# A one-core transformer block on Trainium2: a new order for every job, with new banks and copy engines

## The chip, the cores and the metric

One core of a Trainium2 chip runs the kernel. The metric is the device time of one execution in microseconds, from its start to its end. The engines are TensorE (PE, matmuls and their weight loads), VectorE (DVE), ScalarE (ACT), GpSimd (POOL) and SyncE (SP), whose queue issues all DMAs of this kernel. SBUF is the on-chip memory, and PSUM, 8 banks of 128x512 f32, takes what TensorE writes.

## The reference

Two residual blocks on x of 2048 tokens and 448 columns, bf16. The first is attention with 16 heads of 28 columns, where each token sees 8 keys, at distances 0, 2, ..., 14 behind it. The second is a gated MLP whose gate is mixed over the tokens by a 2048x2048 matrix.

```python
x = A_x
h = x + _A_ref(_layernorm(x, axis=-1), A_wqkv, A_wo)      # attention over 8 keys, then @ wo
h2 = h + _B_ref(_layernorm(h, axis=-1), B_w_in, B_w_sp, B_b_sp, B_w_out)

def _B_ref(x, w_in, w_sp, b_sp, w_out):
    z = _gelu(jnp.einsum('bsd,df->bsf', x, w_in))          # 1792 columns
    z1 = z[..., :Fh].copy()                                # Fh = 896
    z2 = _layernorm(z[..., Fh:], axis=-1)
    g = jnp.einsum('ts,bsf->btf', w_sp, z2) + b_sp[None, :, None]
    return jnp.einsum('bsf,fd->bsd', z1 * g, w_out)
```

## The kernel before

The 2048 tokens are 16 tiles of 128, numbered 0 to 15. In the order of the data, the stages are:

1. *First layer norm*, a tile at a time: statistics on VectorE (L607, tile `st1`), their aggregate (L609, `mv1`), the reciprocal root on GpSimd (L601, L602, `rs`, for groups of one, two or four tiles), and the normalisation on VectorE (L618), which writes `xn`, a ring of six places. The name `n0_5` is the normalisation of tile 5 in layer norm 0.
2. *Transposes of `xn` into `xhT`*: tiles 0 to 3 on TensorE (L647) with an evacuation from PSUM, the others by a DMA from SP's queue (L519).
3. *Projections* (L495, function `product`): queries and keys for five stretches of tokens (256, 256, 512, 512, 512) in four groups of heads each, and V for each attention block. Each product is two jobs, A and B, on half arrays of 64 rows (64\*128 in the profile); another job must stand between them. A function `move` (L505) copies each out of PSUM, on ScalarE or VectorE. The same function makes the padded weights `wqk` out of `wraw` at the start; GpSimd clears their padding (L668).
4. *Attention*, in 18 blocks of 128, 112 or 114 tokens: logits (L763), exponential on ScalarE (L772, tile `E`), the multiplication by the mask on VectorE (L778), the product with V (L787), a reciprocal (L795) and a multiplication (L798) on VectorE into `otm`, a small copy of `otm` (L505), and a DMA transpose into `OT` (L519; through `OTs` and one more copy for blocks that end off a boundary). Then the output projection (L495) and the residual add on VectorE, two tiles at a time (L731), into `x_tm`.
5. *Second layer norm* of these, like the first, and a DMA transpose into `hnT`.
6. *Gate half of the MLP*, for each tile: product (L495), for some tiles a raw copy out of PSUM (L505) with the gelu behind it (L836), for others the gelu straight from PSUM (L839), two halves of statistics (L843, `st3`), aggregate (L846), root on GpSimd, normalisation (L852) into `z2p`.
7. *Other half* (L495 and gelu L880), into `z1p`.
8. *Spatial product* (L908): 28 groups of 16 matmuls of 128x512 with `wsp_la`, `wsp_hi`, `wsp_lb` as weights' sides and the normalised gate `z2p`; then an add of the bias (L917) and the gate's multiplication (L920) on VectorE.
9. *Last projection* (L932), residual add (L939) and the store of the result (L520).

These stages overlap widely: while the attention of later tokens runs, the MLP of the earlier ones has begun. Nothing decides this while the kernel runs or is built: every job (912 of them) has a number, and three lists written out at the top of the file hold the whole arrangement. `ORDER` is the order of all jobs. Each engine issues its own in this order, and waits by semaphores where an operand or a bank isn't ready. The number 912 in it stands for one filler matmul on a constant tile (L947, `warm`). `BANK` has the first PSUM bank of each product in the order in which the products were declared, and `ON` the engine of each copy that may go to either of two.

```python
for t, b in zip(self.tickets, BANK):      # L301
    t.b = b
for i in ORDER:
    j = self.jobs[i]
    out.append(j)
...
eng = ON.get(name, eng)                   # L504, in move
```

Names of copies in `ON`: `xe` evacuates a transpose of `xn`, `wp` pads weights, `qe2_1` evacuates group 1 of the third stretch of queries and keys, `ve` V of a block, `od` copies `otm`, `oc` copies from `OTs` to `OT`, `z2c5` is the raw copy of tile 5's gate.

Of the kernel before, what the change touches and what calls it, by code (L numbers as in the profile page):

```python
# [25 lines left out]
ORDER = [21, 36, 112, 24, 22, 25, 0, 37, 38, 1, 44, 45, 35, 39, 40, 46, 47, 2, 116, 3, 121, 23, 912, 912, 912, 912, 912, 912,  # L26
# [200 lines left out]
class Planner:  # L227
# [69 lines left out]
    def order(self):  # L297

        ready, out = {}, []
        left = [j.ndep for j in self.jobs]  # L300
# [707 lines left out]
```

## Time and profile before

| | |
|---|---|
| three runs | 240.85, 243.95, 241.71 us; median 241.71 |
| profiled execution | 240.89 us, its span 239.2 us |
| TensorE busy | 231.4 us (97%), 2099 matmuls |
| TensorE weight loads | 114.3 us (48%), 2110 |
| VectorE busy | 152.3 us (64%), 323 instructions |
| ScalarE busy | 92.0 us (38%), 113 |
| GpSimd busy | 35.2 us (15%), 73 |
| DMA | 23.26 MB, mean 97 GB/s |

The span runs from the first to the last instruction of the profiled execution; the time has 1.7 us more around it. Weight loads overlap matmuls. An engine's share is a mean over all stages, so it doesn't tell which stage waits for what: for that, the profile is read by stretches of time.

In the rows of the profile, a time line reads: start, duration, engine, line, operation, output and inputs, the number of instructions in the row, and in brackets the idle time ahead of it and what released it. The chain of waits is followed back from the last instruction.

### The profile page before, as it was taken

What the parts mean: (1) busy time and instruction counts of PE and PEld (TensorE: products, weight loads), DVE (VectorE), ACT (ScalarE), POOL (GpSimd) and SP (SyncE); (2) the same over time, 40 slices, a digit from 0 to 9 for tenths busy, and PEclk for the clock granted to TensorE, in tenths of its full rate; (3) what the DMA queues carried; (4) which work ended last, traced back from release to release, by engine and by line L of the source; (5) the groups of instructions that cost most, each with busy time, mean ns of one, the idle gap of its engine ahead of it and who ended that gap; (6) DMA issues with size and microseconds to landing.
All of it is one profiled execution on the core that took longest, in us unless ns stands there. A gap on an engine that the chain in (4) does not pass through costs nothing.

```text
span 239.2 us, 4969 instructions
## 1 busy us (share of the span) xinstructions
PE 231.4 (97%) x2099; PEld 114.3 (48%) x2110; DVE 152.3 (64%) x323; ACT 92.0 (38%) x113; POOL 35.2 (15%) x73
## 2 busy tenths in 40 slices
PE   7989999799999999999999999999999999999995
PEld 2564464354555644444444444444444444444453
DVE  5799799979989987959877124410751222613674
ACT  3787988768789656687820000000000000000000
POOL 5154220440302030313124000000000000000000
DMA  6943538526668967979999970000000010000032
GB/s 202 340 119 69 137 70 142 89 60 124 148 106 165 171 108 157 154 149 165 168 192 166 186 189 0 3 0 0 0 0 3 31 47 0 0 3 0 26 108 97
DMA packets 66310, 23.26 MB, mean 97 GB/s; under 512 B 58608, under 2 KB 66160, under 8 KB 66288
## 3 DMA queue, kind: packets, MB, share of 16 engines
q1 hardware_dynamic: 66288, 22.95, 47.1%
q8 instruction: 16, 0.26, 0.4%
q14 instruction: 6, 0.05, 0.1%
HBM read 6.83 MB, written 1.84 MB: 36 GB/s over the span
## 4 chain that ended last, share of the span: by engine, by line
PE 81%; DVE 9%; DMA 4%; ACT 2%; SPq 2%; issue 1%; POOL 0%
PE psum L908 40%; PE psum L495 27%; PE psum L932 9%; DMA x_tm<-in_A_x_dram 3%; PE psum L763 2%; PE psum L787 2%; DVE st L607 2%; DVE E L778 2%; DMA xhT<-xn 2%; ACT E L772 1%; DVE z2p L505 1%; DVE otm L798 1%; SPq L520 1%; SPq L519 1%; DVE xn L618 1%
## 5 line engine op out<-in xcount | busy, mean ns | idle before, releaser
L908 PE MATMUL psum<-wsp_hi,z2p 128*128 128x512 bf16 x218 | 50.6, 379 | 0.3
L917 DVE TENSOR_TENSOR ub<-psum,bb 128x512 bf16<-128x512 f32 x28 | 19.2, 689 | 44.4 <-PE psum L908 43.9
L772 ACT ACTIVATE E<-psum 128x896 bf16<-128x896 f32 (+2 forms) x36 | 32.0, 934 | 9.0 <-PE psum L763 9.0
L908 PEld LDWEIGHTS psum<-wsp_hi,z2p 128*128 128x128 bf16 x224 | 21.9, 98 | 26.1
L495 PE MATMUL psum<-xhT,wqk 64*128 64x512 bf16 (+1 forms) x280 | 27.1, 334 | 2.0 <-DMA xhT<-xn 1.6
L908 PE MATMUL psum<-wsp_lb,z2p 128*128 128x512 bf16 x108 | 26.1, 379 | 0.2
L908 PE MATMUL psum<-wsp_la,z2p 128*128 128x512 bf16 x111 | 25.9, 379 | 0.2 <-issue 0.2
L495 PE MATMUL psum<-w_in,hnT 64*128 64x448 bf16 x224 | 24.8, 349 | 0.1
L495 PE MATMUL psum<-hnT,w_in 64*128 64x512 bf16 x196 | 24.1, 376 | 0.0
L939 DVE TENSOR_TENSOR srg<-psum,x_tm 128x448 bf16<-128x448 f32 (+1 forms) x17 | 9.7, 592 | 20.8 <-PE psum L932 20.7
L932 PE MATMUL psum<-w_out,z1p 128*128 128x448 bf16 (+1 forms) x119 | 22.3, 341 | 0.0
L843 DVE BATCH_NORM_STATS2 st<-z2p 128x6 f32<-128x448 bf16 x32 | 18.9, 609 | 3.7 <-ACT z2p L836 3.4
L778 DVE TENSOR_TENSOR E<-E,maskb 128x1792 bf16<-128x1792 bf16 (+2 forms) x18 | 19.6, 1095 | 1.7 <-ACT E L772 1.6
L607 DVE BATCH_NORM_STATS2 st<-x_tm 128x6 f32<-128x448 bf16 x32 | 19.4, 612 | 1.6 <-DMA x_tm<-in_A_x_dram 1.4
L602 POOL TENSOR_TENSOR rs<-rs,negh 128x2 f32<-128x2 f32 (+2 forms) x22 | 18.9, 857 | 1.8
L495 PEld LDWEIGHTS psum<-xhT,wqk 64*128 64x128 bf16 x280 | 12.8, 94 | 12.3 <-ACT E L772 2.4
L908 PEld LDWEIGHTS psum<-wsp_la,z2p 128*128 128x128 bf16 x112 | 10.9, 98 | 13.4 <-DVE z2p L852 0.4
L908 PEld LDWEIGHTS psum<-wsp_lb,z2p 128*128 128x128 bf16 x112 | 11.0, 98 | 13.2
L932 PEld LDWEIGHTS psum<-w_out,z1p 128*128 128x128 bf16 x119 | 11.6, 98 | 10.2 <-DVE z1p L920 0.3
L880 ACT ACTIVATE z1p<-psum 128x1024 bf16<-128x1024 f32 x14 | 14.2, 1023 | 5.2 <-PE psum L495 5.1
L495 PEld LDWEIGHTS psum<-w_in,hnT 64*128 64x128 bf16 x224 | 10.6, 94 | 11.0 <-DVE z2p L505 0.6
L601 POOL TENSOR_SCALAR rs<-mv 128x2 f32<-128x2 f32 (+2 forms) x22 | 6.3, 288 | 62.1 <-DVE mv L609 41.3
(54 smaller groups left out, 226.2 us busy)
## 6 DMA issues: line engine op xcount, KB each, us to landing
w_in<-in_B_w_in_dram SPq DMA_DIRECT2D x8, 224.0 KB, 3.0
out_dram<-srg SPq DMA_DIRECT2D x16, 112.0 KB, 1.7
x_tm<-in_A_x_dram SPq DMA_DIRECT2D x3, 448.0 KB, 6.1
wraw<-in_A_wqkv_dram SPq DMA_DIRECT2D x2, 448.0 KB, 4.1
w_out<-in_B_w_out_dram SPq DMA_DIRECT2D x1, 784.0 KB, 6.4
bb<-in_B_b_sp_dram SPq DMA_DIRECT2D x1, 512.0 KB, 5.8
wv<-in_A_wqkv_dram SPq DMA_DIRECT2D x2, 224.0 KB, 6.3
wo<-in_A_wo_dram SPq DMA_DIRECT2D x1, 336.0 KB, 7.7
```

What stands on the lines that cost most here:

```text
L495: ins = e.matmul(out(k), w(k, p0, c), x(k, p0, c), start=(k, p0, c) in first, stop=(k, p0, c) in last, tile_position=(p0, 0))
L601: [(lambda e: e.tensor_single_scalar(A, mv[:, m:m + n, 1], EPS, ALU.add), r_mv[k][m:m + n], [rr]), (lambda e: e.tensor_tensor(R, A, negh[: ...
L602: (lambda e: e.tensor_tensor(R, A, negh[:, 0:1].to_broadcast([128, n]), ALU.pow), [rr, r_negh], r_rs[k][m:m + n])],
L607: [(lambda e: e.bn_stats(st[:, m, :], src), [rsrc], [r_st[k][m]])], dve_t(D))
L772: return e.activation(o, i, AF.Exp, scale=SCALE)
L778: return e.tensor_tensor(a, a, maskb[:, 0:1, pad:pad + nq].to_broadcast([NK, NHEAD, nq]), ALU.mult)
L843: [(lambda e, m=m, k=k: e.bn_stats(st3[:, m, k, :], z2p[:, m, D * k:D * (k + 1)]), [r_z2[m]], [r_st[2][m]])], dve_t(D))
L880: return e.activation(o, i, AF.Gelu_apprx_tanh)
L908: ins = e.matmul(psv(tk), z2p[:, s, 128 * fc:128 * fc + 128], w[:, 512 * (tc % 2):512 * (tc % 2) + 512], start=(s == 0), stop=(s == NB - 1))
L917: [(lambda e, tc=tc, s=s, tk=tk: e.tensor_tensor(ub[:, s, :], psv(tk), bb[:, 512 * tc:512 * tc + 512], ALU.add), [r_bb], [r_ub[s]])], dve_ ...
L932: ins = e.matmul(psv(tk, 0, c1 - c0), z1p[:, fc, 128 * m:128 * m + 128], w_out[:, fc, c0:c1], start=(fc == 0), stop=(fc == FC7 - 1))
L939: [(lambda e, m=m, s=s, tk=tk, c0=c0, c1=c1: e.tensor_tensor(srg[:, s, c0:c1], psv(tk, 0, c1 - c0), x_tm[:, m, c0:c1], ALU.add), [r_x[m]], ...
```

## The change

All three lists are replaced; no other line differs. A line of each as an example:

```diff
-ORDER = [21, 36, 112, 24, 22, 25, 0, 37, 38, 1, 44, 45, 35, 39, 40, 46, 47, 2, 116, 3, 121, 23, 912, 912, 912, 912, 912, 912,
+ORDER = [21, 36, 23, 35, 24, 0, 37, 22, 25, 38, 39, 1, 2, 112, 114, 44, 45, 46, 116, 40, 47, 3, 118, 120, 119, 113, 912, 912,
...
-BANK = [0, 2, 3, 2, 6, 4, 0, 2, 2, 6, 6, 2, 0, 6, 2, 2, 6, 6, 6, 0, 2, 4, 0, 6, 0, 4, 0, 1, 4, 0, 0, 4, 2, 4, 0, 2, 6, 4, 1,
+BANK = [0, 2, 4, 5, 4, 0, 2, 6, 4, 4, 6, 6, 2, 4, 6, 0, 2, 0, 6, 0, 4, 6, 0, 4, 2, 0, 0, 4, 2, 2, 1, 0, 4, 0, 0, 0, 4, 6, 2,
...
-ON = {'xe0_0': 'act', 'xe0_1': 'act', 'xe1_0': 'act', 'xe2_0': 'act', 'xe3_0': 'dve', 'wp0_0_0': 'act', 'wp0_1_0': 'act',
+ON = {'xe0_0': 'act', 'xe0_1': 'dve', 'xe1_0': 'act', 'xe2_0': 'act', 'xe3_0': 'act', 'wp0_0_0': 'act', 'wp0_1_0': 'act',
...
```

The work stays the same, but for 15 filler matmuls at the start where there were 13. In `ON`, these copies go from ScalarE to VectorE: `xe0_1`, `wp0_1_2`, `wp1_1_0`, `qe3_0`, `qe3_2`, `ve2`, `oc15`, `z2c5`, `z2c8`. From VectorE to ScalarE go `xe3_0`, `wp1_1_2`, `qe1_1`, `qe1_2`, `oc12`, `oc14`, `oc17`, `z2c2`, `z2c3`, `z2c6`, `z2c7`. Of the eighteen small copies `od`, six go from VectorE to GpSimd (0, 4, 8, 9, 13 and 14) and five the other way (1, 2, 5, 12 and 16), so that GpSimd has eleven instead of ten. On GpSimd the clearing of the padding (L668) moves from the head of its list to a place between the roots of tiles 0 and 1. The products of the gate's and the other half come in another order of tiles, and with other banks.

Three places follow, as the engines' own lists show them: line, operation, output and inputs, size, and x with the number of equal ones in a row. The first is VectorE's list near its start, in the first layer norm (`st1`, `mv1`, and `xn` for a normalisation). Before, with the statistics of tiles 3 and 2 already behind it, the list goes on with those of tiles 5, 7, 6 and 4, an aggregate after each, and then the normalisations of tiles 3 and 2:

```order
L607 BN_STATS st1_61<-x_tm_49 128x6
L609 BN_AGGR mv1_62<-st1_61 128x2
L607 BN_STATS st1_61<-x_tm_49 128x6
L609 BN_AGGR mv1_62<-st1_61 128x2
L607 BN_STATS st1_61<-x_tm_49 128x6
L609 BN_AGGR mv1_62<-st1_61 128x2
L607 BN_STATS st1_61<-x_tm_49 128x6
L609 BN_AGGR mv1_62<-st1_61 128x2
L618 TENSOR_SCALAR xn_55<-x_tm_49,mv1_62,rs0_67 128x512 x2
L505 CAST xhT_76<-psum 128x4x128
```

After, an evacuation of tile 0's transpose and a padding of weights come first, then the statistics of tiles 2 and 3, those of 7 and 4, and the normalisations of tiles 2 and 3:

```order
L505 CAST xhT_76<-psum 128x2x128
L505 COPY wqk_77<-wraw_83 128x2x8x28
L607 BN_STATS st1_61<-x_tm_49 128x6 x2
L609 BN_AGGR mv1_62<-st1_61 128x2 x2
L607 BN_STATS st1_61<-x_tm_49 128x6 x2
L609 BN_AGGR mv1_62<-st1_61 128x2
L618 TENSOR_SCALAR xn_55<-x_tm_49,mv1_62,rs0_67 128x512 x2
L607 BN_STATS st1_61<-x_tm_49 128x6
```

The statistics of tiles 5 and 6 and one aggregate moved from ahead of these two normalisations to behind them, and the evacuation of tile 3's transpose left VectorE.

The second place is SP's queue where it turns from loads to transposes: `xhT` is a transpose of normalised x, `OT` one of an attention block, `w_in` a load of weights. Before (the eight are tiles 5, 4, 6, 7, 9, 11, 10, 8, the ninth is tile 12, and the last three are 15, 14, 13):

```order
L519 DMA_TRANSPOSE xhT_76<-xn_55 128x4x128 x8
L520 DMA w_in_51<-in_B_w_in_dram 128x896 x2
L519 DMA_TRANSPOSE OT_85<-otm_56 128x4x128
L519 DMA_TRANSPOSE OT_85<-otm_56 128x4x112 x2
L520 DMA w_in_51<-in_B_w_in_dram 128x896 x2
L519 DMA_TRANSPOSE xhT_76<-xn_55 128x4x128
L519 DMA_TRANSPOSE OT_85<-otm_56 128x4x112 x2
L519 DMA_TRANSPOSE xhT_76<-xn_55 128x4x128 x3
L519 DMA_TRANSPOSE OT_85<-otm_56 128x4x112 x2
L520 DMA w_in_51<-in_B_w_in_dram 128x896
L519 DMA_TRANSPOSE hnT_50<-xn_55 128x8x128
```

After (tiles 5, 4, 6, 7, then 10, 9, 8, 11, then 12, 15, 14, and 13 last):

```order
L520 DMA w_in_51<-in_B_w_in_dram 128x896
L519 DMA_TRANSPOSE xhT_76<-xn_55 128x4x128 x4
L520 DMA w_in_51<-in_B_w_in_dram 128x896
L519 DMA_TRANSPOSE xhT_76<-xn_55 128x4x128 x4
L520 DMA w_in_51<-in_B_w_in_dram 128x896
L519 DMA_TRANSPOSE xhT_76<-xn_55 128x4x128 x3
L519 DMA_TRANSPOSE OT_85<-otm_56 128x4x112
L519 DMA_TRANSPOSE OT_85<-otm_56 128x4x128
L519 DMA_TRANSPOSE xhT_76<-xn_55 128x4x128
L519 DMA_TRANSPOSE OT_85<-otm_56 128x4x112 x2
L519 DMA_TRANSPOSE wsp_la_53<-in_B_w_sp_dram 128x1024
L519 DMA_TRANSPOSE OT_85<-otm_56 128x4x112
```

Between the transposes of tiles 5 and 13 there stood five transposes of attention blocks (0, 1, 2, 4 and 3) and four loads of weights; now there stand two transposes of blocks (1 and 0) and two loads, and a transpose of the spatial matrix has come behind it. The normalisations that feed them on VectorE stand together in the same way.

The third place is VectorE's list in the gate's layer norm (`st3`, `mv3`, and `z2p` for a normalisation), a little ahead of the spatial product. Before (the four normalisations in one row are tiles 1, 0, 4 and 5, and the statistics ahead of them belong to tile 8):

```order
L843 BN_STATS st3_65<-z2p_57 128x6 x2
L852 TENSOR_SCALAR z2p_57<-z2p_57,mv3_66,rs2_69 128x896
L843 BN_STATS st3_65<-z2p_57 128x6
L852 TENSOR_SCALAR z2p_57<-z2p_57,mv3_66,rs2_69 128x896 x4
L843 BN_STATS st3_65<-z2p_57 128x6
L846 BN_AGGR mv3_66<-st3_65 128x2
L843 BN_STATS st3_65<-z2p_57 128x6 x6
L846 BN_AGGR mv3_66<-st3_65 128x2 x2
L852 TENSOR_SCALAR z2p_57<-z2p_57,mv3_66,rs2_69 128x896
```

After (the first normalisation is tile 4; then come statistics of tile 12 and both of tile 15, the normalisation of tile 8, one of tile 14, the aggregate of tile 15, and the normalisation of tile 5):

```order
L852 TENSOR_SCALAR z2p_57<-z2p_57,mv3_66,rs2_69 128x896
L843 BN_STATS st3_65<-z2p_57 128x6 x3
L852 TENSOR_SCALAR z2p_57<-z2p_57,mv3_66,rs2_69 128x896
L843 BN_STATS st3_65<-z2p_57 128x6
L846 BN_AGGR mv3_66<-st3_65 128x2
L852 TENSOR_SCALAR z2p_57<-z2p_57,mv3_66,rs2_69 128x896
L843 BN_STATS st3_65<-z2p_57 128x6 x2
L846 BN_AGGR mv3_66<-st3_65 128x2 x2
L843 BN_STATS st3_65<-z2p_57 128x6
L846 BN_AGGR mv3_66<-st3_65 128x2
L843 BN_STATS st3_65<-z2p_57 128x6
L852 TENSOR_SCALAR z2p_57<-z2p_57,mv3_66,rs2_69 128x896
```

Tile 5's normalisation left its place next to those of tiles 1, 0 and 4 and moved behind four more statistics, one aggregate and the normalisation of tile 8.

More of the change, by code (lines that the diff above doesn't have):

```diff
@@ L75 @@
 WINB = 2
-ON = {'xe0_0': 'act', 'xe0_1': 'act', 'xe1_0': 'act', 'xe2_0': 'act', 'xe3_0': 'dve', 'wp0_0_0': 'act', 'wp0_1_0': 'act',
[4 rows of a table removed]
-    'act', 'qe4_3': 'dve', 've0': 'act', 'od0': 'dve', 'od1': 'pool', 've2': 'act', 'od2': 'pool', 'od3': 'pool',
-    've4': 'act', 'od4': 'dve', 'od5': 'pool', 've6': 'dve', 'od6': 'dve', 'od7': 'pool', 've8': 'act', 'od8': 'dve',
-    'od9': 'dve', 've10': 'act', 'od10': 'pool', 'od11': 'pool', 'oc11': 'dve', 've12': 'act', 'od12': 'pool', 'oc12':
-    'dve', 'od13': 'dve', 'oc13': 'act', 've14': 'act', 'od14': 'dve', 'oc14': 'dve', 'od15': 'dve', 'oc15': 'act',
-    've16': 'act', 'od16': 'pool', 'oc16': 'dve', 'od17': 'pool', 'oc17': 'dve', 'z2c1': 'act', 'z2c2': 'dve', 'z2c3':
-    'dve', 'z2c4': 'act', 'z2c5': 'act', 'z2c6': 'dve', 'z2c7': 'dve', 'z2c8': 'act', 'z2c9': 'act', 'z2c10': 'act',
+ON = {'xe0_0': 'act', 'xe0_1': 'dve', 'xe1_0': 'act', 'xe2_0': 'act', 'xe3_0': 'act', 'wp0_0_0': 'act', 'wp0_1_0': 'act',
[4 rows of a table added]
+    'act', 'qe4_3': 'dve', 've0': 'act', 'od0': 'pool', 'od1': 'dve', 've2': 'dve', 'od2': 'dve', 'od3': 'pool',
+    've4': 'act', 'od4': 'pool', 'od5': 'dve', 've6': 'dve', 'od6': 'dve', 'od7': 'pool', 've8': 'act', 'od8': 'pool',
+    'od9': 'pool', 've10': 'act', 'od10': 'pool', 'od11': 'pool', 'oc11': 'dve', 've12': 'act', 'od12': 'dve', 'oc12':
+    'act', 'od13': 'pool', 'oc13': 'act', 've14': 'act', 'od14': 'pool', 'oc14': 'act', 'od15': 'dve', 'oc15': 'dve',
+    've16': 'act', 'od16': 'dve', 'oc16': 'dve', 'od17': 'pool', 'oc17': 'act', 'z2c1': 'act', 'z2c2': 'act', 'z2c3':
+    'act', 'z2c4': 'act', 'z2c5': 'dve', 'z2c6': 'act', 'z2c7': 'act', 'z2c8': 'dve', 'z2c9': 'act', 'z2c10': 'act',
     'z2c13': 'act'}
```

94 rows, old and new, of tables (BANK, ON, ORDER) are left out of this document.

## The prediction

> **What bounds the kernel now.** I read the page first, then the chain, then TensorE by time, then each stretch by engine.
>
> ```profile
> span 239.2 us, 4969 instructions
> PE 231.4 (97%) x2099; PEld 114.3 (48%) x2110; DVE 152.3 (64%) x323; ACT 92.0 (38%) x113; POOL 35.2 (15%) x73
> DVE  5799799979989987959877124410751222613674
> ```
>
> TensorE is at work in 97% of the span, and VectorE's 64% is two different things: near nine tenths in the first half, little in the second. The chain shows where they meet.
>
> ```profile
> 43.18 4.03 DMA xhT<-xn
> 47.41 1.04 PE psum L495 x8
> 118.70 10.74 PE psum L908 x49
> 225.93 10.63 PE psum L932 x63
> ```
>
> From 118.70 on (I call this start of the spatial product G) the chain is TensorE alone, to 236.6. An order cannot shorten that part, since the same matmuls run; it can only break it. Whatever the change gives must be gained before G, in the waits of TensorE. These are the ones to see:
>
> ```profile
> 7.65 3.32 PE L495 MATMUL psum<-xhT,wqk 64*128 64x256 bf16 x56 [0.34 <-ACT xhT L505]
> 12.74 0.72 PE L647 MATMUL psum<-ident,xn 128*128 128x128 bf16 x8 [0.80 <-DVE xn L618]
> 47.41 1.04 PE L495 MATMUL psum<-xhT,wqk 64*128 64x512 bf16 x8 [1.62 <-DMA xhT<-xn]
> ...
> 9.36:84.25 74.89, 72.39 (x1164) 39.47 (x1162) 68.73 (x142) 59.47 (x71) 19.97 (x35) 1.00 0.62 126
> 9.36:118.44 109.08, 106.47 (x1496) 55.47 (x1492) 96.72 (x208) 84.11 (x99) 27.13 (x50) 1.00 0.71 133
> 7.65:118.70 111.05, 108.28 (x1523) 57.01 (x1525) 98.05 (x213) 85.71 (x104) 27.57 (x51) 1.00 0.71 137
> 118.70:236.60 117.90, 117.31 (x556) 55.24 (x565) 49.59 (x100) 2.62 (x3) 4.23 (x8) 1.00 0.24 52
> ```
>
> The last four rows give the length of a stretch, then the busy time of TensorE, weight loads, VectorE, ScalarE and GpSimd. Between the first projection (7.65) and G, TensorE is idle 111.05 - 108.28 = 2.77 us: 0.80 for normalised x, 1.62 for a transpose, 0.35 in small pieces. That is 1.2% of the kernel. VectorE is nearly as full: from 9.36 to 84.25 it is idle 6.16 of 74.89 us, up to 118.44 it is 12.36 of 109.08. So it is the second bound, and a TensorE that waits less runs into it.
>
> **The change part by part.** All sums are against the profiled execution, 240.89 us (span 239.17 and 1.7 around it); the median of three runs is 241.71, 0.8 above it.
>
> *Start.* After, GpSimd clears the weight padding between the two first reciprocal roots, not ahead of all.
>
> ```profile
> 0.79 0.53 POOL L668 MEMSET wqk<- 128x512 bf16 x1 [0.29 <-POOLq L993]
> 5.55 0.41 DVE L618 TENSOR_SCALAR xn<-x_tm,mv,rs 128x512 bf16<-128x512 bf16 x1 [0.47 <-POOL rs L602]
> 6.91 0.60 ACT L505 ACTIVATE xhT<-psum 128x512 bf16<-128x512 f32 x1
> 9.36 0.63 DVE L607 BATCH_NORM_STATS2 st<-x_tm 128x6 f32<-128x448 bf16 x1 [0.61 <-DMA x_tm<-in_A_x_dram]
> 12.30 0.70 DVE L618 TENSOR_SCALAR xn<-x_tm,mv,rs 128x512 bf16<-128x512 bf16 x2
> ```
>
> The clearing took 0.53 and pushes the second root, so the second xn comes near 6.1 instead of 5.55. ScalarE reads its transpose from about 7.15 (6.91 before), because three copies of weights now stand ahead. The first projection starts near 7.9: +0.25. In return xn for tiles 2 and 3 no longer waits for the statistics of tiles 5 and 6: after the load lands at 9.36 only two statistics run ahead (tiles 7 and 4), not four, so 12.30 becomes near 11.0. TensorE comes there at 7.9 + 3.3 + 0.9, about 12, and the 0.80 goes. Net -0.55.
>
> *The last quarter of x.* The 1.62 at 47.41 ends with the transpose issued last of the twelve. Before, its four normalisations were spread between the mask multiplies of six blocks; now they stand together behind four of these. VectorE has twelve statistics (6.6), twelve aggregates (1.2), fourteen normalisations (4.6), an evacuation of V (1.0) and four mask multiplies (4.3) from 9.36 to there, starts apart: 17.7 and some 0.4 of waits, so 27.5. Six transposes follow one another; at 1.27 each the last is issued at about 34 and lands 2.5 to 4 later.
>
> ```profile
> L519 SPq DMA_TRANSPOSE xhT<-xn x12: 1202/1267/2351, 14.4 to 43.2; - x12
> DMA to landing us min/median/max: 2.4/2.5/4.3
> ```
>
> These rows give the issue and the time to landing. That is 36.4 to 38. TensorE, which gets to this projection seven microseconds earlier in its new order (about 37), waits 0 to 1. I take 0: the wait goes, but it is no full gain, as the next part decides.
>
> *VectorE up to the residual add of tiles 10 and 11* (L731). TensorE's later job, the projection of tile 4 for the gate, writes the banks which that add frees. Before, the add ended at 84.25:
>
> ```profile
> 83.19 1.06 DVE L731 TENSOR_TENSOR x_tm<-psum,x_tm 128x896 bf16<-128x896 f32 x1
> ...
> L505 DVE CAST z2p<-psum 128x896 bf16<-128x896 f32 x4 | 4.3, 1084 | 2.0 <-PE psum L495 2.0
> L505 DVE CAST qkT<-psum 128x512 bf16<-128x512 f32 x2 | 1.4, 682 | 0.0
> L505 DVE CAST qkT<-psum 128x1024 bf16<-128x1024 f32 x1 | 1.2, 1225 | 0.0
> L505 DVE CAST V<-psum 128x896 bf16<-128x896 f32 x1 | 1.1, 1092 | 0.0
> L505 DVE COPY OT<-OTs 128x456 bf16<-128x456 bf16 x5 | 1.3, 257 | 0.0
> L505 DVE COPY otm<-otm 112x64 bf16<-112x64 bf16 x4 | 0.7, 182 | 0.0
> L505 DVE CAST xhT<-psum 128x512 bf16<-128x512 f32 x1 | 0.7, 691 | 0.2 <-PE psum L647 0.2
> L843 DVE BATCH_NORM_STATS2 st<-z2p 128x6 f32<-128x448 bf16 x32 | 18.9, 609 | 3.7 <-ACT z2p L836 3.4
> L852 DVE TENSOR_SCALAR z2p<-z2p,mv,rs 128x896 bf16<-128x896 bf16 x16 | 7.4, 493 | 2.2 <-POOL rs L602 2.2
> ```
>
> Up to that add VectorE now also does two large q/k evacuations (2 x 1.225), one more of V (1.09) and a reciprocal (0.25): 3.8. It no longer does two raw z2 copies (2 x 1.084), two small q/k evacuations (2 x 0.682), the xhT copy (0.69), one z2 statistic (0.61), an OT copy (0.26) and a small otm copy (0.18): 5.3. Five instructions fewer overlap 0.08 less each, which gives back 0.4. Net -1.1. Of the 6.16 idle I let 1.4 go; this is my choice, from two rows:
>
> ```profile
> 27.12 1.09 DVE L778 TENSOR_TENSOR E<-E,maskb 128x1792 bf16<-128x1792 bf16 x1 [1.63 <-ACT E L772]
> 48.98 0.26 DVE L795 RECIPROCAL rcp<-psum 112x16 f32<-112x16 f32 x1 [0.79 <-PE psum L787]
> ```
>
> The 0.79 follows the 1.62 wait and goes with it; of the 1.63 I take 0.6, since the exponentials now run ahead of the evacuations but V's evacuation is a new wait. The add then ends at 84.25 - 1.1 - 1.4 = 81.75. The bounds are nothing saved (83.15) and 4 saved (79.15).
>
> *From there to G.* In the new order 356 half-array matmuls are left, 154 of 512 columns and 202 of 448. Starts give their pace:
>
> ```profile
> 111.95 0.92 PE L495 MATMUL psum<-w_in,hnT 64*128 64x448 bf16 x8
> 112.71 1.03 PE L495 MATMUL psum<-hnT,w_in 64*128 64x512 bf16 x8
> 113.57 0.73 PE L495 MATMUL psum<-w_in,hnT 64*128 64x448 bf16 x6
> ```
>
> 0.76 for eight is 0.095 each, 0.86 for eight is 0.1075: 202 x 0.095 + 154 x 0.1075 = 35.75. From 81.85 that puts G at **117.6, 1.1 before the present 118.70**.
>
> *The end of normalisation.* G's fifth group is the first to need tiles 4 to 7, 16 matmuls of 3.45 us in all behind the start: at 121.05. Tile 5's normalisation now stands behind both statistics of tile 15 and one of tile 14. Before, it ended at 118.44:
>
> ```profile
> 116.67 1.76 DVE L852 TENSOR_SCALAR z2p<-z2p,mv,rs 128x896 bf16<-128x896 bf16 x4
> 114.34 0.92 ACT L839 ACTIVATE z2p<-psum 128x896 bf16<-128x896 f32 x1 [1.16 <-PE psum L495]
> ```
>
> Ahead of it come six more statistics on balance (3.65), two normalisations (0.99), three aggregates (0.6), and the exchanges above with the two later raw copies that ScalarE takes over (-2.2 for copies, +2.2 for q/k and V, -1.4 for the rest); less 0.08 for each of six more instructions: +3.4. That is 121.85 with the idle of before and 120.4 with 1.4 less: ready, with 0.6 to spare. Its own chain is as tight: from the end of tile 15's projection, 0.65 ahead of G, 0.2 + 0.92 (gelu) + 1.2 + 0.45 + 0.55 + 0.15 + 0.5 is about 4.0 of the 4.1 that there are. I cost it at 0; bounds 0 and +2.5.
>
> *G to the end.* The same 117.9; VectorE works 49.6 of it. Near the end the adds of tiles 7 and 9 now stand ahead of the last gate multiplies, and these end about when TensorE asks for them: 0 to +0.3, taken as 0.
>
> **Sum: 240.89 - 1.1 = 239.8.** The 0.55 and the 1.62 are not added to it: they are how TensorE reaches the add, and VectorE takes back what is more.
>
> **A rule weighed.** GpSimd's small copies of otm cost very different times:
>
> ```profile
> 29.42 0.24 POOL L505 COPY otm<-otm 112x64 bf16<-112x64 bf16 x1 [4.04 <-DVE otm L798]
> 44.09 1.69 POOL L505 COPY otm<-otm 112x64 bf16<-112x64 bf16 x1
> ```
>
> The second ran beside a mask multiply on VectorE. The Trainium skill, GPSIMD Engine Reference, Specifications, says that the two engines share their SBUF interfaces and contend when VectorE has two SBUF inputs or a two-port mode; the trace agrees. By that rule every copy moved to GpSimd may pay 1.45 more, and a price of 0.24 holds only where VectorE reads PSUM.
>
> The new order has eleven such copies on GpSimd instead of ten, several of them on other tiles, each ahead of a transpose. One late copy on the way to an output projection costs 0 to 0.7, as these transposes have about a microsecond to spare. It speaks against the change and enters the second rival.
>
> **The rivals.**
> 1. *TensorE's waits go altogether*, as VectorE's idle falls by 3 us or more. G then comes at 7.9 + 108.28 = 116.2, which is 238.4; rows shown busy may hide about half as much again (1.4), so down to 237. For it: many of VectorE's waits were for a late TensorE. Against: VectorE had only 6 us of idle. Chance 0.22.
> 2. *Late transposes take the place of the one removed*: at the q/k projection of the last quarter, at the gate's first tiles, or at an output projection behind a slow GpSimd copy. Two landings of 4 instead of 2.5 give back 1 to 2: 240.5 to 241.7, no change. Speaking for it: the 4.03 of the chain. Chance 0.17.
> 3. *Slower: tile 5's normalisation becomes G's gate.* If VectorE is idle as long as before, it ends at 121.85, the fifth group waits 0.8; from about 12.7 us of idle on, 0.3 over before's 12.36, the whole is later than before, each microsecond one for one. With 14 to 15 it ends at 123.5 to 124.5, G in effect at 120 to 121: 242.2 to 243.2. For it: ScalarE takes over two raw copies net, and one late gelu of tile 15 is enough. Against: before, VectorE's large waits in this part were for products that now come earlier. Chance 0.16.
>
> **How the numbers follow.** The forecast, 239.8 with its own range 238.9 to 240.5, has 0.45. I keep 239.8. The range takes in most of rivals 1 to 3 and 0.8 for runs above the profiled one: 237.4 to 242.8. About 2% (4.8 us) is what a measurement of this kernel can tell from no change. Faster by that would need every wait gone and more: 0.04. Slower by that needs two or three of the late mechanisms at once: 0.04. Within it: 0.92.
>
> **What would show it.** First projection near 7.9 and no wait ahead of the transposes of tiles 2 and 3; at most 1 us of TensorE idle before the last q/k quarter; the add of tiles 10 and 11 at 81 to 82.5; G near 117.6 and 117.9 from there to the end of TensorE. It is wrong if TensorE's idle ahead of G does not fall below 2, if a wait stands at the fifth group of G, or if a new gap opens in the last 15 us.

## The result: slower by 0.6%

The change made the kernel slower: a median of 243.28 us over 20 runs (241.90 to 246.21) against 241.94 us for the kernel before (20 runs, 240.68 to 244.26). The ratio is 1.006, with a 95% interval of 1.0038 to 1.0083. Forecast were 239.8 us and a range up to 242.8, so the direction and the range were both missed. A part of the spread goes with TensorE's granted clock: over later jobs the kernel before ran 124 times, 70 at a mean clock of 1.0 (median 241.37 us) and 54 at 0.985 to 0.993 (243.67), and the change, over its three jobs, at 1.0 in 41 of 42 (243.20), so at an equal clock it is about 1.8 us slower.

The profiled execution of the change took 243.36 us. Its page, for the whole span:

```profile
span 241.3 us, 4994 instructions
PE 234.2 (97%) x2112; PEld 115.1 (48%) x2112; DVE 150.6 (62%) x320; ACT 93.3 (39%) x115; POOL 35.4 (15%) x74
DVE  4998869899979976988695044513612063122773
```

At this level nothing has changed: TensorE is busy in 97% of a span that is 2.1 us longer. The stretches between the same landmarks as before (first projection, spatial product, end of TensorE) tell more; the columns are length, then busy time of TensorE, weight loads, VectorE, ScalarE and GpSimd:

```profile
9.36:84.25 74.89, 72.74 (x1155) 39.77 (x1150) 67.09 (x141) 57.71 (x71) 20.55 (x36) 1.00 0.61 123
8.51:84.31 75.80, 73.59 (x1167) 40.52 (x1168) 67.97 (x143) 58.35 (x74) 20.61 (x36) 1.00 0.62 126
84.31:120.52 36.21, 36.04 (x357) 17.08 (x357) 28.79 (x68) 28.84 (x33) 8.22 (x18) 1.00 0.82 162
8.51:120.52 112.01, 109.64 (x1523) 57.60 (x1523) 96.76 (x210) 87.19 (x106) 28.82 (x53) 1.00 0.68 138
120.52:238.80 118.28, 118.20 (x569) 55.19 (x567) 48.80 (x97) 2.21 (x3) 2.99 (x6) 1.00 0.23 47
```

The first projection starts at 8.51 instead of 7.65 (+0.86). From there to the spatial product, G, it takes 112.01 instead of 111.05 (+0.96): TensorE's idle time fell from 2.77 to 2.37, but the same 1523 matmuls fill 109.64 instead of 108.28. G starts at 120.52 instead of 118.70, and the rest takes 118.28 instead of 117.90 (+0.38). VectorE, from 9.36 to 84.25, works 1.64 less and is idle 7.80 instead of 6.16.

TensorE's time line shows the start and the wait that is new:

```profile
6.77 0.72 PE L647 MATMUL psum<-ident,xn 128*128 128x128 bf16 x8 [0.51 <-DVE xn L618]
8.51 3.26 PE L495 MATMUL psum<-xhT,wqk 64*128 64x256 bf16 x56 [0.16 <-ACT xhT L505]
12.46 0.62 PE L647 MATMUL psum<-ident,xn 128*128 128x128 bf16 x8
21.50 0.74 PE L495 MATMUL psum<-wv,xhT 64*128 64x448 bf16 x6
23.10 1.25 PE L495 MATMUL psum<-xhT,wqk 64*128 64x512 bf16 x10 [0.85 <-DMA xhT<-xn]
```

The wait of 0.80 for normalised x at tiles 2 and 3 is gone (12.46 has none), and so is the 1.62 for the last quarter. In their place, TensorE waits 0.85 ahead of the third q/k stretch, at 23.10, for a transpose. The chain of waits names it, and two more like it:

```profile
18.93 4.03 DMA xhT<-xn
22.96 0.14 issue
23.10 5.57 PE psum L495 x50
...
66.75 4.00 DMA OTs<-otm
...
83.40 3.64 DMA OTs<-otm
```

The first is tile 7. In the profile before, its transpose was issued at 18.36 and landed at 20.84, after 2.48. Now it is issued at 18.93 and takes 4.03. VectorE's time line has the rest, its start, its stop behind the second of these transposes, and the ends that the prediction named:

```profile
6.11 0.28 DVE L505 COPY wqk<-wraw 128x448 bf16<-128x448 bf16 x1 [1.67 <-POOL rs L602]
6.30 0.73 DVE L618 TENSOR_SCALAR xn<-x_tm,mv,rs 128x512 bf16<-128x512 bf16 x2
70.77 0.28 DVE L505 COPY OT<-OTs 128x456 bf16<-128x456 bf16 x1 [1.03 <-DMA OTs<-otm]
83.19 1.06 DVE L731 TENSOR_TENSOR x_tm<-psum,x_tm 128x896 bf16<-128x896 f32 x1
123.58 0.46 DVE L852 TENSOR_SCALAR z2p<-z2p,mv,rs 128x896 bf16<-128x896 bf16 x1
```

The add of tiles 10 and 11 ends at 84.25, to the hundredth where it ended before, though VectorE had less to do up to it.

**Why tile 7's transpose took 4.03.** The profile counts transfers of code (queue 8, 16 KB each). In the stretch of tile 7's transpose there was one after the change, and none before; the row of GB/s has 40 equal slices of the stretch:

```profile
GB/s 178 239 223 227 211 215 223 215 169 87 34 5 0 0 0 0 0 0 0 0 70 169 231 211 231 227 202 223 206 202 95 38 9 0 0 0 0 0 0 0
q1 hardware_dynamic: 1066, 0.26, 50.8%
...
GB/s 201 221 229 213 211 142 34 0 0 0 0 0 53 198 224 224 216 213 140 197 0 0 0 0 0 107 160 178 178 125 302 267 338 302 160 71 53 18 46 165
q8 instruction: 1, 0.02, 1.4%
```

The first two rows are before, 18.36 to 20.84 us; the others after, 18.93 to 22.96. A transpose moves its data in two bursts. In the second stretch they are over by slice 19, 20.9 us, 1.9 us behind the issue as against 2.0 before, and yet the landing is at 22.96. The trace has the landings of its sixteen parts, one for each DMA engine:

```
before  20.71 20.71 20.72 20.73 20.75 20.76 20.76 20.77 20.77 20.77 20.78 20.79 20.79 20.80 20.81 20.84
after   21.32 21.34 21.35 21.36 21.38 21.39 21.40 21.42 21.43 21.44 21.46 21.47 21.48 21.50 21.51 22.96
```

Fifteen parts land by 2.6 us after the issue, and one at 4.03. The code transfer started at 20.88, in one packet that lasted 0.91 and so ended at 21.79, 1.17 ahead of the late landing. The trace doesn't name the DMA engine of a packet; that one engine had the code ahead of the last small write of its part is inferred. The Trainium skill, DMA: Bandwidth & Descriptors, Queues, rings and completion order, says that a DMA engine serves its queues in turn but finishes a whole packet before it changes; the trace fits this, with one part of sixteen 1.45 us behind the others. The other profiles taken below bear it out. In ten of the twenty, a code packet starts 1.8 to 2.0 us behind the issue of tile 7's transpose: fifteen parts land by 2.6 us, and the last 0.9 to 1.2 us behind the end of the packet. In the other ten no packet starts between 0 and 2.3 us behind the issue, and the transpose lands in 2.48 to 2.56. So a transpose that is under way when code is fetched can land 1.5 to 1.9 us late. One late part is not the only form of it: for the transpose at 66.75, with a code transfer at 68.62, all sixteen parts are late, the first landing after 3.80 and the last after 4.00; why is open.

### The profile page after: what moved, and what is told of

Same layout as the page of the kernel before. It is cut to its first block, busy times and chain, and to the rows that moved or that the text cites. A ratio compares the mean times of both kernels' runs of the same rounds, so it can differ in the third digit from the quotient of the medians.

```text
span 241.3 us, 4994 instructions
## 1 busy us (share of the span) xinstructions
PE 234.2 (97%) x2112; PEld 115.1 (48%) x2112; DVE 150.6 (62%) x320; ACT 93.3 (39%) x115; POOL 35.4 (15%) x74
## 4 chain that ended last, share of the span: by engine, by line
PE 78%; DVE 11%; DMA 7%; POOL 2%; issue 1%; SPq 1%; DVEq 0%; POOLq 0%
PE psum L908 40%; PE psum L495 25%; PE psum L932 9%; DMA OTs<-otm 3%; DVE st L607 3%; DMA wraw<-in_A_wqkv_dram 2%; PE psum L787 2%; DVE E L778 2%; DMA xhT<-xn 2%; PE psum L763 2%; POOL rs L602 1%; DVE x_tm L731 1%; DVE xn L618 1%; DVE otm L798 1%; DVE mv L609 1%
## 5 line engine op out<-in xcount | busy, mean ns | idle before, releaser
L908 PE MATMUL psum<-wsp_hi,z2p 128*128 128x512 bf16 x224 | 49.3, 379 | 0.0
L495 PE MATMUL psum<-w_in,hnT 64*128 64x448 bf16 x224 | 24.3, 349 | 0.3 <-issue 0.2
L607 DVE BATCH_NORM_STATS2 st<-x_tm 128x6 f32<-128x448 bf16 x32 | 18.6, 611 | 1.1 <-DMA x_tm<-in_A_x_dram 0.9
L778 DVE TENSOR_TENSOR E<-E,maskb 128x1792 bf16<-128x1792 bf16 (+2 forms) x18 | 19.1, 1095 | 0.0
L601 POOL TENSOR_SCALAR rs<-mv 128x2 f32<-128x2 f32 (+2 forms) x22 | 6.8, 308 | 61.2 <-DVE mv L609 38.9
```

Source lines behind the costliest of these rows:

```text
L495: ins = e.matmul(out(k), w(k, p0, c), x(k, p0, c), start=(k, p0, c) in first, stop=(k, p0, c) in last, tile_position=(p0, 0))
L601: [(lambda e: e.tensor_single_scalar(A, mv[:, m:m + n, 1], EPS, ALU.add), r_mv[k][m:m + n], [rr]), (lambda e: e.tensor_tensor(R, A, negh[: ...
L607: [(lambda e: e.bn_stats(st[:, m, :], src), [rsrc], [r_st[k][m]])], dve_t(D))
L778: return e.tensor_tensor(a, a, maskb[:, 0:1, pad:pad + nq].to_broadcast([NK, NHEAD, nq]), ALU.mult)
L908: ins = e.matmul(psv(tk), z2p[:, s, 128 * fc:128 * fc + 128], w[:, 512 * (tc % 2):512 * (tc % 2) + 512], start=(s == 0), stop=(s == NB - 1))
```

## The experiments

**The change and the kernel before, profiled again.** No edit.

> The changed kernel once more, for a second profile of it: what of its time line is the program's and what is chance. If the order itself is the cause, the first projection comes near 8.5 us again, transposes that last 4.0 instead of 2.5 us sit at the same places (the one of tile 7 near 18.9, that of block 11 near 66.8), the add of tiles 10 and 11 ends within 0.4 of 84.25, and the time is 0.4 to 0.8% above before. If chance made the profile, these differ by 1 us or more.

> The kernel before once more, for a second profile. Its first profile, 240.89 us, lies at the fast end of its runs (240.6 to 244.3). If executions differ by where code fetches fall, this profile has other transposes stretched than the first, always beside a fetch, and another wait or two of TensorE of 0.5 to 1.5 us; if they differ by the clock or by loads, the same transposes are slow and all stages are longer alike.

> The kernel before a third time. If it has two kinds of executions, by whether a code fetch near 20.5 to 21.8 us meets tile 7's transpose, this profile is either near 240.9 with tile 7 landing in 2.5 us and no wait at the third q/k stretch, or near 243 with 4 us and a wait near 1.4; nothing between.

Measured: the change again 243.44 us, ratio 1.0065 (1.0036 to 1.0094), G at 120.44, the add ending at 84.20, tile 7's transpose 4.45 with a fetch at 20.49, a wait of 1.3, and the first projection at 8.11, not near 8.5. The slow transpose is the program's and not chance. The kernel before is another matter. Its second profile took 243.05 us:

```profile
PE psum L495 <- DMA xhT<-xn: 2.0, 1, 2.0
PE psum L947 <- DVE warm L576: 1.5, 1, 1.5
PE psum L495 <- ACT V L505: 1.3, 1, 1.3
```

The fetch came at 20.53 instead of 21.84, met tile 7's transpose (4.14 us, landed 22.69), and TensorE waited 1.3 there, at 22.83, and 2.0 for the last quarter. (The row names ScalarE's copy of V, which ended at 22.81; but in the first profile the same projection ran at 21.20 with this copy still under way, so it needs the transpose and not the copy.) The third profile took 243.83 us, at a mean granted clock of 0.992; tile 7 landed in 2.49 there, its fetch at 22.42, and instead tile 8's took 3.77 beside a small code transfer at 28.86 and a wait of 1.3 followed. Then the last quarter was waited for once more, and the clock fell in one slice of its page:

```profile
48.94 1.04 PE L495 MATMUL psum<-xhT,wqk 64*128 64x512 bf16 x8 [1.95 <-ACT E L772]
PEclk9999999979999999999999999999999999999999
```

(The row names ScalarE, but tile 13 landed at 48.73, as far ahead of the row as it was in the first profile.) The trace has the granted clock at a half from 50.48 to 53.89, which is worth an estimated 1.7 us (half of 3.41); the first two profiles have no such stretch. "Either near 240.9 or by tile 7 near 243" was too simple: which transpose is met differs by execution. What stands is that the profile on which the prediction was built was the fortunate one of three. G came at 118.70 in it, and at 120.87 and 121.42 in the others. In all three TensorE waits for the last quarter: 1.62, 2.03 and 1.95.

**Moving the fetches alone.**

```diff
-[e.matmul(psv(tkw), warm[:, 0:128], warm[:], start=True, stop=True) for _ in range(1)]
+[e.matmul(psv(tkw)[:, 128*q:128*q+128], warm[:, 0:128], warm[:, 128*q:128*q+128], start=True, stop=True) for q in range(4)]
```

> Each filler matmul of 512 columns is four of 128: the same columns, but 45 matmuls more stand ahead in TensorE's code, so that each 16 KB code fetch comes some 2.5 us earlier against the work. If fetches are what stretches a transpose that is under way, the slow transposes move to other tiles, always within 2 us of a fetch: tile 7's, 4.0 before, lands in about 2.5 and the 0.86 us of waiting ahead of the third q/k stretch goes, as does the 4.0 of block 11's; the time then falls by 0.5 to 1.5 us. If the neighbouring loads stretch them, the same transposes stay slow and the time stays within 0.3 us of the change.

> The same split of the fillers in the kernel before. If fetches stretch transposes, those of tiles 14 and 13 (4.29 and 4.03 us) change: the fetch that came at 43.90 comes near 41.4, tile 13 lands in less than 3 us and of the 1.62 us of TensorE's wait at most 0.6 is left, unless tile 15 or 14 takes it over; the time falls by 0 to 1.2 us. If loads or the queue stretch them, the wait of 1.6 stays and the time is within 0.3 us.

Measured: 245.87 us, ratio 1.0155 (1.0105 to 1.0204), for the change; 245.28 us, 1.0144 (1.0109 to 1.0179), for the kernel before. The first projection starts at 8.50 and 7.87, as without the edit, so the fillers themselves cost nothing that counts. The fetches moved, and the slow transposes with them. In the change the one of 20.88 came at 18.20: it met tiles 4 and 6 (4.30 and 3.37 us), tile 7 landed in time and the wait ahead of the third q/k stretch went, as expected. Block 11's stayed slow (3.55 instead of 4.00), which had not been expected. Others were met for them: block 4 (4.31), tile 13 (4.27), block 10 (4.06), block 12 (4.69), block 15 (4.67). In the kernel before it came at 20.16 and met tile 7, another at 36.39 met block 2:

```profile
PE psum L495 <- DMA OT<-otm: 2.4, 2, 1.7
PE psum L947 <- DVE warm L576: 1.5, 1, 1.5
PE psum L495 <- ACT V L505: 1.4, 1, 1.4
```

In this kernel the wait for the last quarter went and tile 14 landed in 2.50, but tile 13 took 4.27, beside code transfers at 46.49 and 47.25. The mechanism was told right and the sign wrong: they lost 2.4 us (against same, 243.44) and 3.0 us (against 242.28). The clock isn't the reason: all six executions of the shifted change were at 1.0, and the two of the shifted kernel before that were took 244.25 and 245.28. With all jobs, banks and engines the same, the places of the fetches alone are worth more than the change is. Both orders stand better with the fetches where they are than with this shift; this says nothing of other shifts.

**The start put back.**

```diff
 VectorE: mv0_1
-  wp0_1_2 n0_0 n0_1
+  n0_0 n0_1 wp0_1_2
 GpSimd: wpad from between the roots of tiles 0 and 1 to the head
```

> Only VectorE's and GpSimd's starts are put back as before: the padding copy that waits for a load comes behind the two first normalisations, and GpSimd clears the padding first. If the lost 0.86 us at the first projection matters, it starts near 7.8 and the whole is 0.5 to 0.8 us faster than the change (ratio to before near 1.003). If VectorE is the bound behind it, the projection starts earlier all the same and the time stays within 0.2 us of the change.

Measured: 242.93 us, ratio 1.0064 (1.0034 to 1.0093). The transposes of tiles 0 and 1 came at 5.57 instead of 6.77, but the first projection at 8.44: it now waited 1.08 for ScalarE, whose evacuation of the transpose stands behind three padding copies, and these behind a load of weights. That load landed between 5.41 and 6.49 in the twenty profiles, always issued at 1.7, so a part of the 0.86 at the start is chance. Counted from the landing, the first projection came after 2.44 here and after 2.50 in the change: the edit gains 0.06 at the start, since ScalarE's list is the later of the two. Beside the change in the same job (243.44) the median is 0.51 lower, but the ratios are the same (1.0064 and 1.0065), so no gain is shown.

**The two orders cut and joined.**

```diff
-ORDER = after
+ORDER = after[:187] + [i for i in before if i not in after[:187]]     # head_after
+ORDER = before[:187] + [i for i in after if i not in before[:187]]    # head_before
+ORDER = after[:377] + ...                                             # mid_after
+ORDER = before[:381] + ...                                            # mid_before
```

> The first 187 entries of the new order (to about 27 us, with their banks and engines), then all that is left in the order of before. If the new order loses in its head, at its start and at the stretched transpose of tile 7, it is as slow as the change: 243.2 to 243.6, ratio 1.004 to 1.007. If it loses behind 27 us, it is within 0.4 us of before.

> The first 187 entries of before (to about 28 us), then the rest in the new order. If the head loses, this is as fast as before or faster: 241.5 to 242.5, since the new order keeps its early transposes of the last quarter. If the loss lies behind, it stays at 243 to 243.8. A worse time than both would say that the two parts don't fit each other, and settle nothing.

> The new order up to about 63 us (377 entries), then the order of before. If all of the loss lies ahead of 63 us: 243.2 to 243.6. If it lies behind, where VectorE waits about 1 us for the stretched transpose of block 11 and the residual adds of tiles 8 and 10 come late: 241.8 to 242.5.

> The order of before up to about 63.6 us (381 entries), then the new order. If all of the loss lies ahead of 63 us: as fast as before, 241.8 to 242.5. If it lies behind: 243 to 243.6.

Measured: head_after 242.64 us, 0.9992 (0.9956 to 1.0028); mid_after 243.84, 1.0057 (1.0021 to 1.0092); head_before 247.05, 1.0203 (1.0141 to 1.0265); mid_before 245.91, 1.0157 (1.0096 to 1.0219). The second pair is worse than both kernels, also where the clock stayed at 1.0 (245.63 to 246.41, and 244.79), and settles nothing. The first pair would put the loss between 27 and 63 us, but head_after has tile 7's slow transpose too, and a wait of 1.15 at it, so by the profile it should have lost. Its equal ratio is in part the clock: all its executions were at 1.0, but only 9 of the 23 of the kernel before in this job. Against the median of these, 242.19, head_after lies 0.45 higher, and mid_after, by its ten at 1.0, 1.56. That would put some of the loss ahead of 27 us and more of it behind, but on few executions. Joined orders mix a place with a misfit; I took no more from them.

**Tiles 4 to 7 earlier.** The part of the new order that delays these transposes is undone, and on GpSimd the root of tiles 4 to 7 goes ahead of three masks.

```diff
 VectorE: st0_7 st0_4 mv0_7
-  n0_2 n0_3 st0_6 mv0_6 st0_5 mv0_4 mv0_5
+  st0_6 mv0_6 st0_5 mv0_4 mv0_5 n0_2 n0_3
 GpSimd: mask1 mask2
-  mask3 mask4 mask5 rs0_4
+  rs0_4 mask3 mask4 mask5
```

> The changed kernel, with the statistics of tiles 5 and 6 and their aggregates put back ahead of the normalisations of tiles 2 and 3 (as before), and three of the masks of GpSimd behind the root of tiles 4 to 7. The transposes of tiles 4 to 7 are issued about 0.8 us earlier. If the code fetch near 20.9, which meets tile 7's transpose, is what costs, tile 7 lands in 2.5 us, near 20.6, the wait of 1.0 to 1.5 ahead of the third q/k stretch goes, 0.4 to 0.8 of waiting for normalised x comes back, and the time falls by 0.3 to 0.9 us. If VectorE's total work sets the end, the time stays within 0.2.

> The first edit again (statistics of tiles 5 and 6 back ahead of the normalisations of tiles 2 and 3). If it takes away the main loss, its median lies 0.7 to 1.3 us below that of the change in the same job; if the first comparison was luck of the chip, within 0.4 us.

Measured: 242.41 us, ratio 1.0006 (0.9964 to 1.0049), and in a second job 242.26 us, 1.0056 (1.0018 to 1.0093). In the first profile:

```profile
span 240.2 us, 4983 instructions
20.18 0.93 PE L495 MATMUL psum<-wv,xhT 64*128 64x448 bf16 x8 [0.19 <-ACT E L772]
21.05 0.40 PE L763 MATMUL psum<-qkT 28*128 28x112 bf16 x16
21.37 0.74 PE L495 MATMUL psum<-wv,xhT 64*128 64x448 bf16 x6
21.95 2.32 PE L495 MATMUL psum<-xhT,wqk 64*128 64x512 bf16 x20
```

The third q/k stretch starts at 21.95 without a wait. Tile 7 was issued at 18.35 and landed at 20.91, though the fetch came at 20.74, 2.39 behind the issue: that is past the point at which it does harm. The wait for normalised x that was to come back (0.4 to 0.8) didn't. The add of tiles 10 and 11 ended at 83.10, and G came at 119.60, in the second profile at 83.10 and 119.25, about 1.1 ahead of the change. Beside the change in one job (below) the medians differ by 0.67 us, just under the least that had been expected, but by the ratios (1.0056, and 1.0043 for the change) the edit gains nothing, and its two ratios don't agree with each other. So the profile shows the mechanism, and the times of one job don't show the gain clear of noise. At a clock of 1.0 on both sides its medians lie 0.98 and 1.12 above before: a good part of the loss is still there.

**VectorE's stop at block 11.**

```diff
 VectorE: mv1_6
-  oc11 mv1_7 st1_4 st1_5 mv1_5
+  mv1_7 st1_4 st1_5 mv1_5 oc11
```

> The changed kernel, with VectorE's copy of block 11 out of OTs put behind two statistics and two aggregates of the second layer norm, so that VectorE has 1.5 us of work while that block's transpose, stretched to 4.0 us by a fetch, is under way. If VectorE's stop of 1.0 us there is what makes the later masks and adds late, the four waits of TensorE of 0.25 to 0.5 us between 76 and 88 shrink by half or more, the add of tiles 10 and 11 ends near 83.3, and the time falls by 0.5 to 1.0 us. If not, the time stays within 0.2 us.

> Both of these edits. If they are two separate losses, the gains add: 0.8 to 1.9 us below the change, so 241.5 to 242.6, as fast as before. If the later one is a consequence of the earlier one, it gains no more than the better of the two.

> The changed kernel beside the next two on one chip, so that they can be compared directly: near 243.4 again, its profile with tile 7's transpose at 4.0 to 4.5 us and a wait of 1.0 to 1.5 ahead of the third q/k stretch.

> The second edit alone again. Its profile showed the loss at tile 7 unchanged and a new stop at block 15 for the one removed; by that its median is within 0.4 us of the change. If the stop at block 11 costs by itself, it lies 0.5 us or more below.

Measured: oc_later 242.88 us, 1.0014 (0.9977 to 1.0052); both 242.26 us, 0.9984 (0.9945 to 1.0022); and side by side on one chip, same_2 (the change) 242.93 us, 1.0043 (1.0002 to 1.0083), norms_back_2 242.26, oc_later_2 243.81, 1.0051 (1.0012 to 1.0089). The second edit does what it says, and gives it back 8 us later:

```profile
71.19 0.25 DVE L505 COPY OT<-OTs 128x456 bf16<-128x456 bf16 x1
79.67 0.62 DVE L798 TENSOR_TENSOR otm<-psum,rcp 114x448 bf16<-114x448 f32 x1 [1.59 <-DMA OTs<-otm]
```

The stop of 1.03 at 70.77 is gone, and VectorE, that much earlier, stops 1.59 at block 15's multiplication, whose place in the ring of three is still being read by block 12's transpose: 4.20 us, met by the fetch at 77.28. Tile 7 was met as in the change, the add ended at 84.86 instead of the expected 83.3, and G came at 121.01.

**Block 12's transpose first.**

```diff
 SP: oT11
-  oT13 whi9 whi2 oT12
+  oT12 oT13 whi9 whi2
```

> The changed kernel with both edits and a third: the transpose of block 12 is issued ahead of that of block 13 and of two transposes of the spatial matrix, so some 4 us earlier. If VectorE's stop of 2.2 us at the multiplication of block 15 (which writes the place that block 12's transpose still reads) is what gave the second edit's gain back, it goes, the wait of 1.9 ahead of an output projection falls below 0.6, and the time falls by 0.7 to 1.5 us below the kernel with both edits: ratio to before 0.990 to 0.996. If another wait is right behind it, the ratio stays at 0.996 to 1.001.

> The first and the third edit without the second: VectorE's copy of block 11 stays where the change put it. If the stop at block 11's stretched transpose counts for itself, this is 0.4 to 1.0 us slower than the kernel with all three. If only the stop at block 15 counted, both are the same within 0.3 us.

Measured: 241.99 us, 0.9986 (0.9954 to 1.0017), with all three edits; 241.95 us, 0.9999 (0.9963 to 1.0035), without the second. The stop at block 15 went in both, yet all three edits give no more than two (0.9984), and the kernel with the stop at block 11 left in is as fast. So neither stop on VectorE could be shown to cost time in the end. No version was clearly faster than the kernel before.

Taken together: five runs with the first edit (norms_back twice, both, three, norms_oT12) have medians of 241.95 to 242.41, their mean 242.17; six with tile 7's transposes as the change has them (the change, same, same_2, start_back, oc_later twice) 242.88 to 243.81, their mean 243.21. Tile 7 landed in 2.55 or 2.56 us in all five profiles of the first kind, and in 3.99 to 4.45 in all six of the second; G came at 119.15 to 120.17 in the first, and at 120.36 to 122.07 in the second. These runs are of several jobs and chips, but neither the medians nor the starts of G overlap.

## Why the prediction was wrong

**The step that failed: VectorE's idle time up to the add.** "Of the 6.16 idle I let 1.4 go" put the add of tiles 10 and 11 at 81.75. The work ahead of it did shrink, by 1.64 where 1.1 had been worked out; but the idle time rose to 7.80, and the add ended at 84.25. VectorE's waits were taken to be the waits of before for a late TensorE, which would shrink; TensorE was late again for a new reason. With the first edit, which takes that reason away, the add ended at 83.10; so it accounts for about 1.15 of the 2.5 us by which the add missed the forecast, and the rest is not assigned.

**What that reason is.** The new order takes the normalisations of tiles 2 and 3 ahead of the statistics of tiles 5 and 6, and so gains the 0.80. The price was not in the sum: all four transposes of tiles 4 to 7 are issued later (tile 7 at 18.93 instead of 18.36; a part of that is the late load below, and in further profiles of the change it was 18.45 and 18.57). What counts is the code fetch: it comes 1.8 to 2.0 us behind tile 7's issue in every profile of the change and of its variants that keep this order, and meets the transpose, 0.85 to 1.3 us of waiting at TensorE. With the first edit it comes 2.35 us or more behind. The prediction gave a landing of "2.5 to 4" to the last quarter only, where it read 4.03 in the chain, and did not ask why it was 4.03 (fetches at 43.90 and 45.04) nor which other transposes could be met.

**The start.** Forecast was 7.9, measured 8.51, and 8.0 to 8.7 in the further profiles of this order. The size of the step was right, and the rest is chance. In the six profiles that begin in the order of before, the first projection starts 2.24 us behind the landing of the load of weights that the padding copies read; in twelve with the new start, 2.49 or 2.50. So the order costs 0.26, where +0.25 had been forecast, and the other 0.60 of the 0.86 is the load, which landed at 6.01 instead of 5.41. The row at 6.11 shows VectorE's copy of weights waiting for it, with both normalisations queued behind. (The row names GpSimd, whose second root ended at 6.03.)

**The same matmuls are not the same time.** The first rival's 116.2 rested on 108.28 of TensorE for 1523 matmuls, and so did the forecast's idea of what is left. They took 109.64. In part this is the order itself:

```profile
61.24 0.37 PE L763 MATMUL psum<-qkT 28*128 28x114 bf16 x8
61.60 0.93 PE L495 MATMUL psum<-wv,xhT 64*128 64x448 bf16 x8
62.47 0.37 PE L763 MATMUL psum<-qkT 28*128 28x114 bf16 x8
62.77 0.74 PE L495 MATMUL psum<-wv,xhT 64*128 64x448 bf16 x6
...
64.20 0.40 PE L763 MATMUL psum<-qkT 28*128 28x114 bf16 x16
64.53 0.74 PE L495 MATMUL psum<-wo,OT 64*128 64x448 bf16 x6
```

Logits alone between two projections take 0.36 and 0.30 from their start to the next start; two of them together 0.33. The new order has 20 passages from logits to a projection where there were 16. An estimate over all jobs, from start to start at the usual step of each passage, is 0.2 to 0.6 us, by which step is taken as usual. The rest of the 1.36 I put down to small waits inside rows that count as busy, as among the logits from 66.1 on, which take 0.73 where sixteen of them take 0.40 at 64.20; this is argued and not shown.

**What was right.** The wait of 1.62 went, and tile 13 landed at 37.48, within the stated 36.4 to 38. The 0.80 went. The start's +0.25 was right, as said. From the add to G the pace was right: 84.31 plus 35.75 is 120.06, measured 120.52. From G to the end the bound of +0.3 was nearly right at +0.38. Tile 5's normalisation, rival 3's gate, ended at 124.04, later than its upper bound (120.4 + 2.5), but G was late as well and its fifth group needed it at 123.97. The matmul there starts 0.34 behind the one before it, where the usual step is 0.22: a wait of 0.12, too short to be marked in a row. Of the signs of being wrong, TensorE's idle time ahead of G is the one that clearly came: it stayed above 2, at 2.37. The second rival, late transposes in place of the one removed, was the true one in kind. It had 0.17, it didn't name tile 7's place, and its 240.5 to 241.7 are too low even with the 1.05 of the base (below) added.

**The base.** The sum started from 240.89, the fast end of a spread of 240.3 to 244.7, with few above, that the kernel before shows over all jobs, and its other two profiles have G 2.2 and 2.7 later. Much of that spread goes with the granted clock, as the result shows; among executions at 1.0, 240.89 is 0.5 below the median. "0.8 above it" was said of the median and not asked about. Of the error of 3.5 (243.28 less 239.8), 1.05 lies there (241.94 less 240.89); the rest is a forecast gain of 1.1 that was a loss of 1.34.

GpSimd's slow copies, the rule that was weighed, played little part: after the change, two of the eleven took 2.03 (at 39.14) and 1.05 (at 63.37), each beside mask multiplies on VectorE, and the others 0.23 to 0.38. SP's queue was still busy with other transposes when each of the two ended, so none was late for that.

The wait for the last quarter, which the change did remove, may have been worth more than its 1.62. In the twenty profiles TensorE has seven waits of 1.7 to 2.1 us behind the first projection, and five of them are followed, or overlapped, by a stretch of 3.4 us or more at half the granted clock; none of eleven waits of 1.2 to 1.7 is. That would explain why the change keeps its clock and the kernel before often doesn't, but no run tests it.

What stays open: why the fetch near 20 to 22 us comes up to 2 us earlier or later in executions of the kernel before, and where that part of the loss lies that the first edit leaves, about 1 us at an equal clock.

## What to carry to other kernels

When a hand-made order moves the time by less than 1%, look at a second profile of the kernel before you build a sum on the first: ask which waits in it are the program's and which are one execution's, and compare executions of an equal granted clock. A step that is moved forward delays all that it passes, so list the next deadline of each thing passed (here tile 7's transpose, with 0.4 us to spare), not only that of the wait you remove. Where a transfer on the path takes 4 us instead of 2.5, look for what else its DMA engines did in that stretch; a landing has sixteen parts, and the latest counts.

## What the hardware showed

Code transfers of 16 KB, one for about 130 matmuls here, are on the DMA engines that serve the transposes: 3.4 to 4.7 us instead of 2.5 for those named above that they meet, in some through one late part of sixteen (tile 7), in others with all sixteen late (block 11). A shift of these transfers by 39 matmuls in the kernel before and 45 in the change, with the work unchanged, cost 3.0 and 2.4 us of 242. The Trainium skill, Runtime: NRT & Kernel Launch, Instruction fetch mechanics, says that code comes in blocks of 16 KiB, 256 instructions, by DMA, and calls the cost mostly hidden; the trace agrees on the blocks (2112 matmuls and as many weight loads, sixteen blocks), but here the cost shows on the transposes that the fetches meet. Not all that meet are late: one with the fetch 2.39 us behind its issue lands in 2.56 (fetch at 20.74, landing at 20.91).

The granted clock of TensorE fell to a half for 3.41 us, in one such stretch or two on end, in four of the twenty profiles. Each stretch began within, or 0.9 to 1.6 us behind, a wait of TensorE of 1.72 to 2.13 us; two waits of 1.75 and 2.03 had none behind them, so the length alone doesn't decide.
